# Single-token attention on one core: a first load in halves, a later one whole, one copy whole, one scaling on another engine, shorter column groups, and one load cut at row 120

## The chip, the cores and the metric

One core of a Trainium2 chip. The metric is device time in microseconds (us), median of several executions. The kernel before takes 1254.63 us. Its first three executions lie within 0.1 us of each other. "The span" is the stretch from the first to the last instruction in the trace; a run's time is 1.7 to 1.9 us longer.

## The reference

```python
B, H, Sq, Skv, Dh = 8, 32, 1, 4096, 128        # bfloat16 q, k, v
scale = Dh ** -0.5
scores = jnp.einsum('bhqd,bhkd->bhqk', q, k) * scale
attn = softmax(scores, axis=-1)
return jnp.einsum('bhqk,bhkd->bhqd', attn, v)
```

256 heads with one query each. Every byte of K and V (537 MB together) is read once.

## The kernel before

Heads are worked off in 32 tiles of 8. A tile of K or V is `[128 partitions, C = 256 positions, 128]`, 64 KB in each partition, 8.4 MB in all. VectorE multiplies K by q, TensorE sums over d, ScalarE takes exponentials, TensorE multiplies the weights by V. There is one V buffer and two K buffers; the last V goes into a K buffer. The loads and the tail:

```python
    cuts = {
        ("k", 0): [C // 4, C // 4, C // 2],
        ("k", NT - 4): [C // 2] * 2,
        ("k", NT - 3): [C // 2] * 2,
        ("k", NT - 2): [C // 2] * 2,
        ("k", NT - 1): [C // 4, C // 4, C // 2],
        ("v", NT - 1): [C // 2, C // 4, C // 8, C // 16, C // 32, LAST, LAST],   # LAST = 4
    }
    def load(kind, t):
        # ... choose buffer ...
        c0 = 0
        for n in cuts.get((kind, t), [C]):
            nc.sync.dma_start(buf[:, c0 : c0 + n, :], src[t, :, c0 : c0 + n, :])
            c0 += n
            if kind == "k" and t == 0 and c0 == n:
                nc.sync.dma_start(q_all[:], q_n)          # q goes behind the first piece
# ...
    def values_of(t, lo, hi):
        # weights x V, 4 positions a matmul, into one of four groups of 32 columns
        group = [
            0 if t == NT - 1 and C // 2 <= c0 < 3 * C // 4 else c0 // CB % TG
            for c0 in range(0, end, CB)
        ]
# ...
    def copy_of(t):                                       # PSUM -> SBUF, in bf16
        n = CB if t < NT - 1 else CB // 2
        nc.scalar.activation(out=comb[:, 0:n, :], in_=av[:, 0:n, :], func=ACT.Copy)
        if n < CB:
            nc.vector.tensor_copy(out=comb[:, n:CB, :], in_=av[:, n:CB, :])
# ...
    def finish_of(n):                                     # divide by the sum of weights, store
        nc.scalar.activation(out=stages[s][:, u, :], in_=ops.pop(n)[:], func=ACT.Copy,
                             scale=rzs.pop(n)[:, 0:1])
        # ... nc.scalar.dma_start(out ...)
```

The end runs so: the seven pieces of the last V land, the last values are multiplied, the last four positions (`w_last`) go straight into the result, the values are copied, four matmuls with `pick` collect them (`result_of`), the result is scaled and stored.

Of the kernel before, what the change touches and what calls it, by code (L numbers as in the profile page):

```python
# [7 lines left out]
ACT = mybir.ActivationFunctionType  # L8
ALU = mybir.AluOpType
# [6 lines left out]
TG = 4  # L16
# [7 lines left out]
def kernel(  # L24
# [7 lines left out]
    nc = tc.nc  # L32
    B, H, Sq, D = q.shape
    S = k.shape[2]
    P = nc.NUM_PARTITIONS
# [3 lines left out]
    C = S // PH  # L39
    NT = NH // G  # L40
    scale = float(D) ** -0.5
# [4 lines left out]
    CB = 4  # L46
    RG = R * G
    NQ = NT // R
# [28 lines left out]
        out=ident[:], in_=ident[:], pattern=[[-1, P]], compare_op=ALU.not_equal,  # L77
# [6 lines left out]
        out=heads[:], in_=heads[:], pattern=[[-1, G], [0, PH]], compare_op=ALU.not_equal,  # L84
# [6 lines left out]
        out=own[:], in_=own[:], pattern=[[-PH, G]], compare_op=ALU.is_ge,  # L91
# [3 lines left out]
        out=own[:], in_=own[:], pattern=[[PH, G]], compare_op=ALU.is_ge,  # L95
# [5 lines left out]
        out=same[:].rearrange("p (h x) -> p h x", x=PH),  # L101
        in_=own[:].rearrange("p (b h) -> p h b", h=TB // PH)
# [7 lines left out]
    for j in range(TG):  # L110
        part = pick[j * AG : (j + 1) * AG, :, :, :]
        nc.gpsimd.affine_select(
            out=part, in_=part, pattern=[[-G, CB], [G, R], [-1, RG]],
# [3 lines left out]
            out=part, in_=part, pattern=[[-G, CB], [0, R], [0, RG]],  # L117
# [3 lines left out]
            out=part, in_=part, pattern=[[G, CB], [0, R], [0, RG]],  # L121
# [7 lines left out]

    loads = {}  # L130
    cuts = {
        ("k", 0): [C // 4, C // 4, C // 2],
        ("k", NT - 4): [C // 2] * 2,
        ("k", NT - 3): [C // 2] * 2,
        ("k", NT - 2): [C // 2] * 2,
        ("k", NT - 1): [C // 4, C // 4, C // 2],
# [3 lines left out]
    def load(kind, t):  # L140
        src = k_t if kind == "k" else v_t
        home = "v" if kind == "v" and t < NT - 1 else "k"
        pool = k_pool if home == "k" else v_pool
        buf = pool.tile([P, C, D], BF16, name=f"{kind}t", tag=home)
        c0 = 0
        for n in cuts.get((kind, t), [C]):
            nc.sync.dma_start(buf[:, c0 : c0 + n, :], src[t, :, c0 : c0 + n, :])  # L147
            c0 += n
            if kind == "k" and t == 0 and c0 == n:
                nc.sync.dma_start(q_all[:], q_n)  # L150
        assert c0 == C
        loads[kind, t] = buf
# [88 lines left out]
    def values_of(t, lo, hi):  # L241
        vt = loads["v", t]
        w = ws[t]
        if lo == 0:
            avs[t] = ps_v.tile([P, CB * D], F32, name="av", tag="av")
        end = C if t < NT - 1 else C - LAST


        group = [
            0 if t == NT - 1 and C // 2 <= c0 < 3 * C // 4 else c0 // CB % TG  # L250
            for c0 in range(0, end, CB)
        ]
        for c0 in range(lo, hi, CB):
            i = c0 // CB
            j = group[i]
            nc.tensor.matmul(  # L256
                avs[t][j * AG : (j + 1) * AG, :], lhsT=w[:, c0 : c0 + CB, :],
                rhs=vt[:, c0 : c0 + CB, :], start=(i < TG), stop=(j not in group[i + 1 :]),
            )

    ops = {}
    zps = {}
    rzs = {}
    stages = {}
# [15 lines left out]
    def copy_of(t):  # L280
        comb = small.tile([P, CB, D], BF16, name="comb", tag="comb")
        av = avs.pop(t)[:].rearrange("p (m d) -> p m d", d=D)
        n = CB if t < NT - 1 else CB // 2
        nc.scalar.activation(out=comb[:, 0:n, :], in_=av[:, 0:n, :], func=ACT.Copy)  # L284
        if n < CB:
            nc.vector.tensor_copy(out=comb[:, n:CB, :], in_=av[:, n:CB, :])  # L286
        combs[t] = comb

    def result_of(t):
# [16 lines left out]
    def finish_of(n):  # L306
        s, u = divmod(n, OB)
        if u == 0:
            stages[s] = o_pool.tile([RG, OB, D], BF16, name="stage", tag="stage")
        nc.scalar.activation(  # L310
            out=stages[s][:, u, :], in_=ops.pop(n)[:], func=ACT.Copy, scale=rzs.pop(n)[:, 0:1]
        )
        last = s == NQ // OB - 1
        if u == OB - 1 or (last and u == OB - 2):
            lo = u if (last and u == OB - 1) else 0
            nc.scalar.dma_start(o_n[s, :, lo : u + 1, :], stages[s][:, lo : u + 1, :])

    Q = C // 4
    load("k", 0)
    with tc.manual_schedule():  # L320
        q_prep(0)
        for t in range(NT):
            v_last = t >= NT - 2
            n = t // R - 1
            if t + 1 < NT:
                load("k", t + 1)
            load("v", t)
            product(t, 0, Q)
            sum_over_d(t, 0)
            if t > 2 and t % R == 1:  # L330
                recip_of(n)
                finish_of(n)
# [5 lines left out]
            if t > 0 and not v_last:  # L338
                values_of(t - 1, 0, C)
                copy_of(t - 1)  # L340
# [6 lines left out]
            if t > 0 and v_last:  # L347
                values_of(t - 1, 0, C)
            scores_of(t, 3)
            weights_of(t)  # L350
            if t > 0:
                if v_last:
                    copy_of(t - 1)
                if t % R == 0:
                    norm_of(n)
                result_of(t - 1)
        values_of(NT - 1, 0, C // 2)
        norm_of(NQ - 1)
        recip_of(NQ - 1)
        values_of(NT - 1, C // 2, C - LAST)  # L360
        copy_of(NT - 1)
        result_of(NT - 1)
        finish_of(NQ - 1)


# [28 lines left out]
```

## Time and profile before

| | before |
|---|---|
| time, median | 1254.63 us (1254.58 to 1254.67) |
| span | 1252.8 us |
| DMA engines busy | 9 tenths or more in 39 of 40 slices |
| VectorE / TensorE / ScalarE busy | 77% / 44% / 27% |
| mean granted TensorE clock | 0.685 |

The load stream bounds the kernel; every other engine has time to spare. The lines of the profile are in the prediction. Each view has its own form: the chain of waits gives start, length and what was waited for or executed, and is read from the bottom up; the DMA view of a window gives packets, megabytes and the share that these packets took of sixteen engines' time.

### The profile page before, as it was taken

What the parts mean: (1) busy time and instruction counts of PE and PEld (TensorE: products, weight loads), DVE (VectorE), ACT (ScalarE), POOL (GpSimd) and SP (SyncE); (2) the same over time, 40 slices, a digit from 0 to 9 for tenths busy, and PEclk for the clock granted to TensorE, in tenths of its full rate; (3) what the DMA queues carried; (4) which work ended last, traced back from release to release, by engine and by line L of the source; (5) the groups of instructions that cost most, each with busy time, mean ns of one, the idle gap of its engine ahead of it and who ended that gap; (6) DMA issues with size and microseconds to landing.
All of it is one profiled execution on the core that took longest, in us unless ns stands there. A gap on an engine that the chain in (4) does not pass through costs nothing.

```text
span 1252.8 us, 8134 instructions
## 1 busy us (share of the span) xinstructions
PE 554.0 (44%) x3299; PEld 202.6 (16%) x3299; DVE 967.6 (77%) x531; ACT 343.3 (27%) x625; POOL 6.0 (0%) x26
## 2 busy tenths in 40 slices
PE   2444543345534355333453334542445434545356
PEld 0111111111111111111111111111112111211112
DVE  7877887777977779777797777886778877977981
ACT  0333123331233321333213333123330333311333
POOL 1000000000000000000000000000000000000000
PEclk8667666667657767576765776666676766676777
DMA  9999999999999999999999999999999999999997
GB/s 404 435 436 432 434 435 433 434 432 434 435 434 436 434 429 429 431 432 433 434 434 436 430 436 436 436 434 435 432 427 427 437 433 432 434 420 431 430 439 311
DMA packets 11734, 537.53 MB, mean 429 GB/s; under 512 B 1840, under 2 KB 2096, under 8 KB 2352
## 3 DMA queue, kind: packets, MB, share of 16 engines
q1 hardware_dynamic: 11360, 536.94, 99.3%
q8 instruction: 26, 0.43, 0.1%
q10 hardware_dynamic: 336, 0.07, 0.0%
q14 instruction: 12, 0.10, 0.0%
HBM read 536.94 MB, written 0.07 MB: 429 GB/s over the span
## 4 chain that ended last, share of the span: by engine, by line
DMA 79%; PE 14%; DVE 6%; issue 0%; SPq 0%; another core or an unknown queue 0%; ACT 0%
DMA vt<-in_v_dram 78%; PE av L256 13%; DVE kt L175 3%; DVE kt L178 2%; PE ps L190 1%; DMA q_all<-in_q_dram 1%; DVE sc L202 0%; SPq L147 0%; DVE pmax L212 0%; DVE spread L214 0%; DVE nmax L219 0%; DVE comb L286 0%; ACT comb L284 0%; ACT stage L310 0%
## 5 line engine op out<-in xcount | busy, mean ns | idle before, releaser
L175 DVE TENSOR_TENSOR kt<-kt,qb 128x8192 bf16<-128x8192 bf16 x128 | 565.2, 4415 | 181.9 <-DMA kt<-in_k_dram 175.3
L190 PE MATMUL ps<-kt,ident 128*128 128x512 bf16 x1024 | 353.6, 508 | 572.1 <-DVE kt L178 572.1
L231 ACT ACTIVATE w<-sc,bias 128x256 bf16<-128x256 f32 x256 | 300.5, 1587 | 260.5 <-DVE bias L223 260.5
L178 DVE TENSOR_TENSOR kt<-kt 128x4096 bf16<-128x4096 bf16 x128 | 293.4, 2292 | 4.4
L190 PEld LDWEIGHTS <-ident 128*128 128x128 bf16 x1024 | 119.6, 119 | 775.5 <-issue 506.1
L256 PE MATMUL av<-vt,w 128*32 128x512 bf16 x2047 | 176.5, 513 | 90.0 <-DMA vt<-in_v_dram 90.0
L202 DVE TENSOR_REDUCE sc<-ps 128x64 f32<-128x512 f32 x128 | 87.8, 686 | 68.1 <-PE ps L190 68.1
L284 ACT ACTIVATE comb<-av 128x512 bf16<-128x512 f32 (+1 forms) x32 | 19.5, 609 | 413.1 <-PE av L256 413.1
L231 ACT ACTIVATION_READ_ACCUMULATOR w<-sc,bias 128x1 f32 x256 | 126.6, 495 | 0.0
L256 PEld LDWEIGHTS <-w 128*32 128x32 bf16 x2047 | 68.7, 125 | 207.1 <-DMA vt<-in_v_dram 107.8
L163 ACT ACTIVATE qg<-qh 8x128 bf16<-8x128 f32 x32 | 8.5, 266 | 165.9 <-PE qh L159 165.9
L310 ACT ACTIVATE stage<-op,rz 16x128 bf16<-16x128 f32 x16 | 5.9, 371 | 56.4 <-DVE rz L276 41.3
L301 PE MATMUL op<-comb,pick 128*16 128x128 bf16 x128 | 13.4, 230 | 12.8 <-ACT comb L284 12.4
L212 DVE TENSOR_REDUCE pmax<-sc 128x1 f32<-128x256 f32 x32 | 13.4, 420 | 1.1
L165 PE MATMUL qp<-qg,heads 8*128 8x128 bf16 x32 | 7.5, 235 | 12.7 <-ACT qg L163 12.7
L276 DVE RECIPROCAL rz<-zp 16x1 f32<-16x1 f32 x16 | 2.4, 149 | 13.9 <-PE zp L268 13.9
L159 PE MATMUL qh<-q_all,ident 128*8 128x128 bf16 x32 | 8.2, 256 | 8.3 <-DMA q_all<-in_q_dram 8.3
L167 ACT ACTIVATE qb<-qp 128x128 bf16<-128x128 f32 x32 | 8.9, 277 | 10.4 <-PE qp L165 10.4
L301 PEld LDWEIGHTS <-pick 128*16 128x16 bf16 x128 | 7.6, 91 | 21.0 <-issue 20.9
L214 DVE TENSOR_SCALAR spread<-same,pmax 128x32 f32<-128x32 f32 x32 | 7.7, 241 | 1.1
L223 DVE TENSOR_SCALAR bias<-own,nmax 128x8 f32<-128x8 f32 x32 | 7.4, 231 | 1.1
L219 DVE TRANSPOSE_TENSOR_REDUCE nmax<-spread 128x1 f32<-128x32 f32 x32 | 6.8, 211 | 1.1
(27 smaller groups left out, 20.1 us busy)
## 6 DMA issues: line engine op xcount, KB each, us to landing
kt<-in_k_dram SPq DMA_DIRECT2D x8, 4096.0 KB, 43.0
kt<-in_k_dram SPq DMA_DIRECT2D x4, 2048.0 KB, 23.3
vt<-in_v_dram SPq DMA_DIRECT2D x1, 4096.0 KB, 41.4
vt<-in_v_dram SPq DMA_DIRECT2D x1, 2048.0 KB, 45.9
vt<-in_v_dram SPq DMA_DIRECT2D x1, 1024.0 KB, 47.8
vt<-in_v_dram SPq DMA_DIRECT2D x1, 512.0 KB, 48.6
vt<-in_v_dram SPq DMA_DIRECT2D x31, 33.3
kt<-in_k_dram SPq DMA_DIRECT2D x27, 47.4
```

The lines of the kernel that those rows point to most:

```text
L159: nc.tensor.matmul(qh[:], lhsT=ident[:, p0 : p0 + G], rhs=q_all[:, x, :], start=True, stop=True)
L163: nc.scalar.activation(out=qg[:], in_=qh[:], func=ACT.Copy)
L167: nc.scalar.activation(out=qb[:, 0, :], in_=qp[:], func=ACT.Copy)
L175: nc.vector.tensor_tensor(out=part, in0=part, in1=qb[:].to_broadcast([P, MC, D]), op=ALU.mult)
L178: nc.vector.tensor_tensor(out=part[:, :, 0 : D // 2], in0=part[:, :, 0 : D // 2], in1=part[:, :, D // 2 : D], op=ALU.add,)
L190: nc.tensor.matmul(ps[:], lhsT=ident[:], rhs=kt[:, u * UC : (u + 1) * UC, s * DS : (s + 1) * DS], start=(s == 0), stop=(s == n - 1),)
L202: nc.vector.tensor_reduce(out=scs[t][:, u * UC : (u + 1) * UC], in_=sums.pop((t, u))[:], axis=AX.X, op=ALU.add)
L212: nc.vector.tensor_reduce(out=pmax[:], in_=sc[:], axis=AX.X, op=ALU.max)
L231: nc.scalar.activation(out=w[:, :, g], in_=sc[:], func=ACT.Exp, bias=bias[:, g : g + 1], scale=scale, accum_out=esum[:, t % R, g : g + 1],)
L256: nc.tensor.matmul(avs[t][j * AG : (j + 1) * AG, :], lhsT=w[:, c0 : c0 + CB, :], rhs=vt[:, c0 : c0 + CB, :], start=(i < TG), stop=(j not i ...
L284: nc.scalar.activation(out=comb[:, 0:n, :], in_=av[:, 0:n, :], func=ACT.Copy)
L301: nc.tensor.matmul(ops[n][:], lhsT=pick[:, m, r, :], rhs=comb[:, m, :], start=(r == 0 and m == 0), stop=(r == R - 1 and m == CB - 1),)
```

## The change

The intent: fewer DMAs where cutting no longer helps, a shorter tail after the last load, and relief for the one DMA engine that comes last.

```diff
     cuts = {
-        ("k", 0): [C // 4, C // 4, C // 2],
-        ("k", NT - 4): [C // 2] * 2,
+        ("k", 0): [C // 2] * 2,
@@ load
-            nc.sync.dma_start(buf[:, c0 : c0 + n, :], src[t, :, c0 : c0 + n, :])
+            for p0, p1 in ((0, P - 8), (P - 8, P)) if kind == "v" and n == C // 32 else ((0, P),):
+                nc.sync.dma_start(buf[p0:p1, c0 : c0 + n, :], src[t, p0:p1, c0 : c0 + n, :])
@@ values_of
-            0 if t == NT - 1 and C // 2 <= c0 < 3 * C // 4 else c0 // CB % TG
+            0 if t == NT - 1 and C // 2 <= c0 < C // 2 + 3 * C // 16 else c0 // CB % TG
@@ copy_of
-        n = CB if t < NT - 1 else CB // 2
-        nc.scalar.activation(out=comb[:, 0:n, :], in_=av[:, 0:n, :], func=ACT.Copy)
-        if n < CB:
-            nc.vector.tensor_copy(out=comb[:, n:CB, :], in_=av[:, n:CB, :])
+        nc.scalar.activation(out=comb[:], in_=av, func=ACT.Copy)
@@ finish_of
-        nc.scalar.activation(out=stages[s][:, u, :], ..., func=ACT.Copy, scale=rzs.pop(n)[:, 0:1])
+        if n == NQ - 1:
+            nc.vector.tensor_scalar(out=stages[s][:, u, :], in0=ops.pop(n)[:],
+                                    scalar1=rzs.pop(n)[:, 0:1], scalar2=None, op0=ALU.mult)
+        else:
+            nc.scalar.activation(...)                     # as before
```

The diff also takes away the cut of the K of tile 28 (`NT - 4`).

More of the change, by code (lines that the diff above doesn't have):

```diff
@@ L309, in finish_of @@
             stages[s] = o_pool.tile([RG, OB, D], BF16, name="stage", tag="stage")
-        nc.scalar.activation(
-            out=stages[s][:, u, :], in_=ops.pop(n)[:], func=ACT.Copy, scale=rzs.pop(n)[:, 0:1]
-        )
+        if n == NQ - 1:
+            nc.vector.tensor_scalar(
+                out=stages[s][:, u, :], in0=ops.pop(n)[:], scalar1=rzs.pop(n)[:, 0:1],
+                scalar2=None, op0=ALU.mult,
+            )
+        else:
+            nc.scalar.activation(
+                out=stages[s][:, u, :], in_=ops.pop(n)[:], func=ACT.Copy,
+                scale=rzs.pop(n)[:, 0:1],
+            )
         last = s == NQ // OB - 1
```

## The prediction

The sum is 0.64 + 0.13 + 0.04 = 0.81 us, so 1253.82 us. What the term of 0.64 rested on is the assumption, which no trace of before shows, that the 120-row part leaves out the engine that comes last. That engine would then lose its eight packets, 80 ns apart, and the landings from 1246.9 to 1248.00 that the text gives follow from this. Rival (1) is that another engine is left out.

> **What bounds the kernel now.** I read the page first, then the chain of waits, the timeline of both ends, the DMA view in short windows, and at last the trace's single records (matmuls, DMA packets, and the sixteen landing marks of each DMA). From the page:
>
> ```profile
> DMA  9999999999999999999999999999999999999997
> ...
> DMA 79%; PE 14%; DVE 6%; issue 0%; SPq 0%; another core or an unknown queue 0%; ACT 0%
> ```
>
> K and V are read once, 537 MB by the page, and the DMA engines are busy in every slice but the last. In the inner slices they move about 434 GB/s, and 537 MB at 434 GB/s is 1237 us of the 1252.8 us span. No part of the change removes bytes, so only what lies outside that stream can move: about 1.8 us before the first packet (the first starts at 1.83 us) and the end. The chain of waits at the end (start, length, what, in us):
>
> ```profile
> 1199.17 48.80 DMA vt<-in_v_dram
> 1247.97 0.04 issue
> 1248.02 0.73 PE av L256 x3
> 1248.77 0.39 ACT comb L284
> 1249.16 0.02 issue
> 1249.19 0.44 DVE comb L286
> 1249.62 0.04 issue
> 1249.67 0.29 PE op L301 x2
> ```
>
> The 8-column piece of the last V lands at 1247.97, and then 2.4 us of small work follow (the last step, not shown, is ScalarE's scaling at 1249.97); the store and the closing waits take another 2.4 us (issue at 1250.36, span end 1252.77). The DMA view of three short windows near the end, 1244 to 1245, 1246 to 1247 and 1247 to 1248 us (packets, MB, share of 16 engines):
>
> ```profile
> q1 hardware_dynamic: 60, 0.25, 59.8%
> ...
> q1 hardware_dynamic: 151, 0.16, 43.8%
> ...
> q1 hardware_dynamic: 22, 0.03, 7.1%
> ```
>
> 7.1% is one engine in sixteen: the last microsecond is one engine working alone. The sixteen landing marks of the 8-column piece say the same: six engines at 1241.70 to 1242.69, nine at 1246.13 to 1246.87, one at 1247.97. The lone engine's packets of this piece are 8 of 2,048 bytes, 80 ns apart, from 1246.90 to 1247.54; two more pieces of 8 packets of 1,024 bytes follow, 43 ns apart. So the end is set by **one late engine**, 1.1 us behind the next.
>
> Why it is late shows too. The page lists 26 instruction packets (16,384 bytes each); following packets by their ends, each fetch lengthens one load packet beside it by about 0.5 us, eight different engines take turns, and the last fetch before the end (1231.87 us) falls on the engine that comes last. I expect the same fetches after[...].
>
> [...]
>
> **Part by part.**
>
> *First K in halves, instead of two quarters and a half.* The first product needs the first piece and q behind it. It started at 9.57; a quarter is 2.1 MB, 4.8 us at 434 GB/s, so now it starts near 14.4. That moves VectorE by 4.8 us in the first two tiles. SP's own issues before:
>
> ```profile
> 40.98 0.33 SPq L147 DMA_DIRECT2D kt<-in_k_dram  x1
> 66.73 0.33 SPq L147 DMA_DIRECT2D vt<-in_v_dram  x1
> 73.91 0.33 SPq L147 DMA_DIRECT2D kt<-in_k_dram  x1
> ```
>
> The third K goes out at 40.98 while the first V lands only at 61.6, so at 45.8 it is still early. The second V needs the first values done: near 70 instead of 66.7, while the third K transfers until 80.6. The fourth K moves from 73.9 to at most 78.7, needed at 100. No gap in the stream: 0.
>
> *K of tile 28 whole.* The name in the diff is the fourth from last. VectorE's multiplies of tiles 27 and 28 began:
>
> ```profile
> 1053.09 4.42 DVE L175 TENSOR_TENSOR kt<-kt,qb 128x8192 bf16<-128x8192 bf16 x1 [6.90 <-DMA kt<-in_k_dram]
> ...
> 1084.89 4.42 DVE L175 TENSOR_TENSOR kt<-kt,qb 128x8192 bf16<-128x8192 bf16 x1
> ```
>
> Whole tiles land every 38.7 us, so tile 28 starts at 1091.8, 6.9 us later. But in tile 28 VectorE waited 6.1 us at 1118.95 behind values that need a V, so its end moves only about 3 us (1122.5 to 1125.5), and tile 29 waits 6.6 us in the same place (1157.1), so it ends where it did. The K loads behind are issued some 25 us ahead of need. Cost: 0.
>
> *The 120 and 8 split.* [...] The piece then lands with the next engines, 1246.9 plus at most one packet of 0.08; the last two pieces land at 1247.68 and 1248.00 instead of 1248.32 and 1248.64. Its semaphores shift, so the last piece now waits for the V before it to land (1227.9): 20 us early enough.
>
> *Column groups.* In one group matmuls start 0.216 us apart; in four groups, four start together. Before, 16 from 1243.69 plus three of the later pieces ran in a line until 1247.57, 0.2 us after the landing of the 16-column piece (1247.33). With 12 in line and 4 spread, all before that piece has started by 1246.75. The work then follows the landings: 1247.37 for four, 1247.58 for two, 1247.72 for the last (before: 1248.36). By itself the part is worth nothing, since the old kernel waits at 1248.02 anyway; with earlier landings it keeps about 0.07 us from being lost.
>
> *Copy and scaling.* By shape (mean ns after the comma):
>
> ```profile
> L284 ACT ACTIVATE comb<-av 128x512 bf16<-128x512 f32 x31 | 19.1, 617 | 402.8 <-PE av L256 402.8
> ...
> L286 DVE CAST comb<-av 128x256 bf16<-128x256 f32 x1 | 0.4, 424 | 6.6 <-ACT comb L284 6.6
> ```
>
> The halves were meant to run side by side and ran one after the other: VectorE waited for ScalarE. From the last value's end to the last result matmul's end that took 1.20 us (1248.735 to 1249.938). A whole copy takes 0.597 in 29 of 31 cases (the mean holds two of 0.90 right after exponentials); with 0.04 ahead, 0.05 behind, four result matmuls 0.055 apart (0.165) and 0.217 for the last, 1.07: **0.13 saved**. The last scaling on ScalarE took 0.357 in the timeline. VectorE's reciprocal of one element from PSUM took 0.149 and its 256-element cast 0.424, so about 0.28 for 128 elements, perhaps 0.36 with a pointer scalar (bias, 8 elements, takes 0.231): estimate 0.32, **0.04 saved**. The store is issued from ScalarE's queue, which now waits for another engine, at the 0.03 us it waited before.
>
> Sum[...]: 0.64 + 0.13 + 0.04 = 0.81 us. Times of whole runs stand 1.85 us over the span and move with it: 1254.63 - 0.81 = 1253.82.
>
> **Rivals.** (1) [...] Then the landing stays[...], and only 0.17 us remain: 1254.5. I give this 1 in 4. (2) Starting later opens a gap in the stream, because K tile 28 or the first K now frees a buffer late: each gap would cost its length, up to 5 us, 1259. The margins above (some 10 us at the start, 25 at tile 28) speak against it. (3) TensorE, not the landing, is the bound at the end: then the groups part would give the gain, and the split none. The wait at 1248.02 for the landing speaks against it.
>
> **Range.** The three runs before lie within 0.1 us, so differences of half a microsecond are real on one chip. I mix 0.81 (3 in 4) and about 0.15: 1253.9. The range, 1253.0 to 1255.0, holds both outcomes and a little of another chip. 2% is 25 us, thirty times anything in the sum: within 2% is nearly sure.
>
> **What would show it.** Right: first product near 14.4, tile 28 multiplied from about 1091.8, and yet a last V landing no later; the lone engine's tail before 1248 shorter by 0.64; the last value near 1247.7; one copy of 0.60; store issued near 1249.55. Wrong: the last landing unchanged (the engine is another), a DMA share under 9 in an inner slice (a gap), or a VectorE scaling over 0.40 us.

## The result, and the profile after

The changed kernel took 1255.3 us (1255.09 to 1255.53, 6 runs), the kernel before 1254.64 (1254.58 to 1254.67, 6 runs). The ratio is 1.0005 (95% interval 0.9992 to 1.0018). The interval does not separate the two; the runs do, since the ranges don't touch. The change **costs** about 0.7 us, where 0.7 us was to be saved, and 1255.3 lies outside the range.

The chain of waits of the changed kernel at its end (start, length, what):

```profile
1199.12 49.84 DMA vt<-in_v_dram
...
1249.00 0.70 PE av L256 x3
...
1249.72 0.61 ACT comb L283
...
1250.37 0.40 PE op L298 x4
...
1250.79 0.34 DVE stage L308
```

Set it beside the same chain of before: the last three value matmuls begin at 1249.00 and not at 1248.02. The piece whose landing they wait for comes 0.99 us later. The last step of before, which the prediction does not show, was

```profile
1249.97 0.36 ACT stage L310
```

From the values on, the tail is shorter: 1249.00 to 1251.13 (end of the scaling) is 2.13 us, before it was 1248.02 to 1250.33, 2.31 us.

The groups by shape say the same of the two steps that changed engine or size:

```profile
L283 ACT ACTIVATE comb<-av 128x512 bf16<-128x512 f32 x32 | 19.7, 616 | 407.3 <-PE av L256 407.3
...
L308 DVE TENSOR_SCALAR stage<-op,rz 16x128 bf16<-16x128 f32 x1 | 0.3, 339 | 7.2 <-PE op L298 7.2
```

The DMA view of windows 1244 to 1245, 1246 to 1247, 1247 to 1248 and 1248 to 1249 us after (the first three answer to those of before):

```profile
q1 hardware_dynamic: 58, 0.24, 57.9%
...
q1 hardware_dynamic: 149, 0.18, 69.8%
...
q1 hardware_dynamic: 73, 0.07, 22.9%
...
q1 hardware_dynamic: 20, 0.02, 6.5%
```

Between 1246 and 1247 the engines are busy for 69.8% of their time and not 43.8%, for hardly more bytes (0.18 MB against 0.16). They are not idle, they are slow. One engine alone (6.5%) still works in a microsecond that before was nearly empty (1.0% from 1248 to 1249.5 us). TensorE shows the consequence; its timeline:

```profile
1248.40 0.40 PE L256 MATMUL av<-vt,w 128*32 128x512 bf16 x4 [0.90 <-DMA vt<-in_v_dram]
1249.00 0.69 PE L256 MATMUL av<-vt,w 128*32 128x512 bf16 x3 [0.20 <-DMA vt<-in_v_dram]
```

It idles 0.90 us for the 16-column piece, a piece that the change does not touch. So the delay is there before the cut piece. The trace keeps, for each DMA, the times at which its semaphore was counted up, sixteen for a whole one; they are called landing marks here. The last mark of each piece of the last V:

```text
columns of the piece    before     after
128                     1238.72    1238.69
 64                     1243.65    1243.96
 32                     1246.07    1246.59
 16                     1247.33    1248.36
  8 (120 rows after)    1247.97    1248.96
  8 (8 rows)               -       1247.63
  4                     1248.32    1249.27
  4                     1248.64    1249.58
```

Up to 1238.7 the streams are alike, so neither the first K nor tile 28 left a mark there. Then two stretches lose time. The view by windows (length, busy times of the engines, clock, DMA share, GB/s) of 1240.5 to 1242.0, before and then after:

```profile
1240.50:1242.00 1.50, 1.50 (x20) 0.83 (x13) 0.00 (x0) 0.00 (x0) 0.00 (x0) 0.50 0.95 380
```

```profile
1240.50:1242.00 1.50, 1.50 (x20) 0.84 (x16) 0.00 (x0) 0.00 (x0) 0.00 (x0) 0.50 0.99 304
```

Busier (0.99 against 0.95) and slower (304 against 380 GB/s): a fifth less. In single records, the late engine's 16,384-byte packets, 611 to 619 ns each before, took 740, 844 and 656 ns here. In the second stretch, 1246.0 to 1247.5, six of its 4,096-byte packets took 188 to 382 ns instead of 159. These extras add up to 0.39 + 0.57 = 0.96 us. The cut piece is moved in packets of 2,048 bytes. They start from 1240.33 to 1242.44 on the engines that are early and from 1245.46 to 1246.93 on the nine in the middle, and each of the two stretches overlaps one of these.

The records carry no engine number, but the landing marks tell which engines are which. The 120-row DMA has one mark at its issue (1199.73) and fifteen later, the 8-row DMA eight later. Of the fifteen, five are early, nine in the middle, one late. All sixteen are six, nine and one. So the engine that gets nothing is one of the **early** ones. The 8-row part's eight marks are four early and four in the middle; the late engine is not among them. It still has its eight packets of 2,048 bytes (1247.83 to 1248.39, 80 ns apart).

The start and tile 28 answered much as predicted. What SP (SyncE, which issues the loads) issued after:

```profile
45.94 0.33 SPq L147 DMA_DIRECT2D kt<-in_k_dram  x1
69.35 0.33 SPq L147 DMA_DIRECT2D vt<-in_v_dram  x1
79.37 0.33 SPq L147 DMA_DIRECT2D kt<-in_k_dram  x1
```

and VectorE's first multiply and the first of tile 28:

```profile
14.54 4.42 DVE L175 TENSOR_TENSOR kt<-kt,qb 128x8192 bf16<-128x8192 bf16 x1 [11.58 <-ACT qb L167]
...
1091.89 4.42 DVE L175 TENSOR_TENSOR kt<-kt,qb 128x8192 bf16<-128x8192 bf16 x1 [6.81 <-DMA kt<-in_k_dram]
```

### The profile page after: what moved, and what is told of

The parts are those of the page before. It is cut to its first block, busy times and chain, and to the rows that moved or that the text cites. A ratio compares the mean times of both kernels' runs of the same rounds, so it can differ in the third digit from the quotient of the medians. Undisturbed runs are those within 1.5% of the kernel's fastest.

```text
span 1253.5 us, 8130 instructions
## 1 busy us (share of the span) xinstructions
PE 553.9 (44%) x3299; PEld 201.7 (16%) x3299; DVE 967.5 (77%) x531; ACT 343.1 (27%) x624; POOL 6.0 (0%) x26
## 4 chain that ended last, share of the span: by engine, by line
DMA 79%; PE 15%; DVE 6%; issue 0%; SPq 0%; ACT 0%
DMA vt<-in_v_dram 78%; PE av L256 13%; DVE kt L175 3%; DVE kt L178 2%; PE ps L190 1%; DMA q_all<-in_q_dram 1%; DVE sc L202 0%; SPq L147 0%; DVE pmax L212 0%; ACT comb L283 0%; DVE spread L214 0%; DVE nmax L219 0%; PE op L298 0%; DVE stage L308 0%; ACT qb L167 0%
## 5 line engine op out<-in xcount | busy, mean ns | idle before, releaser
L283 ACT ACTIVATE comb<-av 128x512 bf16<-128x512 f32 x32 | 19.7, 616 | 407.3 <-PE av L256 407.3
```

The costliest lines, as they stand in the source:

```text
L283: nc.scalar.activation(out=comb[:], in_=av, func=ACT.Copy)
```

## The experiments

The theory (P), as far as runs can test it: when a load is cut in rows, which rows of SBUF are written at the same time decides how long its packets take, and packets of other DMAs that run beside it take longer too. The mechanism behind this was not shown by any run. The rivals were the shifted compute, the additional DMA, and the number of engines used.

**1. Without the split.** The changed kernel, with

```diff
-            for p0, p1 in ((0, P - 8), (P - 8, P)) if kind == "v" and n == C // 32 else ((0, P),):
-                nc.sync.dma_start(buf[p0:p1, ...], src[t, p0:p1, ...])
+            nc.sync.dma_start(buf[:, c0 : c0 + n, :], src[t, :, c0 : c0 + n, :])
```

> The changed kernel with the 8-column piece whole again; all else of the change stays. Theory P ([...]packets that run at the same time get slower): the 16-column piece of the last V lands near 1247.3 again and not at 1248.36, the 4,096-byte packets take 159 ns throughout, and the time is 1254.63 less the 0.15 that the copy (1.20 to 1.07) and the scaling (0.357 to 0.339) save: 1254.5. Rival K (the shifted start or the whole K of tile 28 moved the stream or the phase of the compute against it): stays at 1255.2 to 1255.4.

1254.28 us (1254.08 to 1254.38, 4 runs) against 1254.49 of before (1254.46 to 1254.63, 7 runs), ratio 0.9998. The loss is gone, and about 0.2 us is saved. The last three values start at 1248.12, and the stretch 1240.5 to 1242.0 runs at 373 GB/s again:

```profile
1240.50:1242.00 1.50, 1.50 (x20) 0.77 (x16) 0.00 (x0) 0.00 (x0) 0.00 (x0) 0.50 0.93 373
```

Whatever the split costs, the rest of the change does not cost it.

**2. The split alone**, in the kernel before (the same lines added).

> The kernel before with the 120 and 8 split alone. Theory P: the last landings come about 1.0 us later as in the changed kernel, and nothing is saved in the tail: 1255.4 to 1255.7. Rival K: as before, 1254.6, or 1254.0 if the split does what the prediction said.

1255.53 us (1255.38 to 1256.24, 4 runs), before 1254.49, ratio 1.0009: about 1.0 us lost, and the 8-column piece lands at 1249.00 (120 rows). So the split alone brings the loss, and the rival of the shifted compute falls. The profiled execution was the slowest, 1256.24, for a reason of its own. TensorE's timeline there:

```profile
1244.16 6.16 PE L257 MATMUL av<-vt,w 128*32 128x512 bf16 x31 [2.02 <-DMA vt<-in_v_dram]
```

31 matmuls in one run without a gap of note, from 1244.16 to 1250.32. Single records show the ones in a line 0.43 us apart for about 3 us instead of 0.216, so in this execution TensorE itself was late. The trace has the reason: the granted TensorE clock (the third column from the right) was about half in that stretch. The view of 1245 to 1248 us, run 2 and then before:

```profile
1245.00:1248.00 3.00, 3.00 (x9) 1.04 (x8) 0.00 (x0) 0.00 (x0) 0.00 (x0) 0.51 0.53 188
```

```profile
1245.00:1248.00 3.00, 2.95 (x23) 1.27 (x22) 0.00 (x0) 0.00 (x0) 0.00 (x0) 1.00 0.38 143
```

That raised the question of runs 13 and 14.

**3. As many DMAs, but whole rows.** Run 1 with the 8-column piece as two of 4 columns:

```diff
-        ("v", NT - 1): [C // 2, C // 4, C // 8, C // 16, C // 32, LAST, LAST],
+        ("v", NT - 1): [C // 2, C // 4, C // 8, C // 16, C // 64, C // 64, LAST, LAST],
```

> The changed kernel with the 8-column piece as two pieces of 4 columns, each over all 128 rows: the same number of DMAs as with the split[...]. Theory P: as without the split, 1254.4 to 1254.7. Rival N (one DMA more, its issue held back until 1227.8, its descriptors and semaphore cost the time): 1255.2 or more.

1254.20 us (1254.16 to 1254.43, 4 runs), ratio 0.9998. One DMA more costs nothing.

**4. The split at 112 and 16 rows.** The changed kernel with

```diff
-            for p0, p1 in ((0, P - 8), (P - 8, P)) if ...
+            for p0, p1 in ((0, P - 16), (P - 16, P)) if ...
```

> The changed kernel with the split at 112 and 16 rows[...]. Theory P: slower than without the split by about as much as the 120 and 8 split, 0.6 to 1.2 us over it: 1255.1 to 1255.7. Rival E (what costs is that 15 and 8 engines are used instead of 16): as without the split, 1254.5.

1255.35 us (1255.07 to 1256.1, 4 runs), ratio 1.0009. As slow as 120 and 8, so the loss does not hang on these two numbers. How many engines each part used here was not shown; that it isn't a matter of fifteen engines instead of sixteen is shown by run 5 below, where all are busy (0.98) and yet slow.

**5 to 8. The cost made large.** Run 1 with the whole V of tile 16, in the middle of the stream, cut in rows. `parts` is the only thing that differs:

```diff
+            parts = PARTS if kind == "v" and t == NT // 2 else [slice(0, P)]
+            for rs in parts:
+                nc.sync.dma_start(buf[rs, c0 : c0 + n, :], src[t, rs, c0 : c0 + n, :])
# run 5: [slice(0, P // 2), slice(P // 2, P)]
# run 6: [slice(0, P - 8), slice(P - 8, P)]
# run 7: [slice(32 * h + r, 32 * h + 32, 4) for h in range(4) for r in range(4)]   8 rows, 4 apart
# run 8: [slice(8 * h, 8 * h + 8) for h in range(16)]                              8 rows in sequence
```

> The changed kernel without the split at the end, but with the whole V of tile 16 in the middle of the kernel loaded as rows 0 to 63 and rows 64 to 127, to see the suspected cost large. [...] Theory P: [...]these packets take about 4.8 us instead of 2.42 and the kernel some 19 us longer (8.39 MB at half of 434 GB/s). [...]

> The same with rows 0 to 119 and 120 to 127 of the V of tile 16. Theory P: most packets of that load take between 2.42 and 4.8 us or more, and the kernel is 10 to 29 us longer. Rival E (only the share of rows per engine counts[...]): 2.4 us longer at most.

> The same V of tile 16 as 16 DMAs of 8 rows each, taken 4 rows apart (rows 0, 4, ... 28 of each 32), so that each is moved by 8 engines[...]. Theory P: packets stay at 2.42 us, but only 8 engines work: 38.8 us instead of 19.3, the kernel about 19 us longer (1274).

> The same as 16 DMAs of 8 consecutive rows. [...]only the order of rows differs. Theory P: [...]packets take about 9.7 us, and the kernel is about 135 us longer (16 packets of 9.7 us instead of 19.3 us). A theory in which the number of engines alone counts: as with rows 4 apart, 1274.

One look each (state unknown), with 1254.62 us for before on the same chip: 1278.07 (64 and 64), 1283.84 (120 and 8), 1288.8 (8 rows 4 apart), 1331.3 (8 rows in sequence). The view by windows, 662 to 682 us, while that V loads; the last two columns are the DMA share and GB/s. First run 1, where it is whole, then runs 5, 6, 7 and 8:

```profile
662.00:682.00 20.00, 7.60 (x18) 2.39 (x18) 17.22 (x7) 6.23 (x13) 0.00 (x0) 0.50 1.00 430
```

```profile
662.00:682.00 20.00, 4.02 (x11) 1.42 (x12) 13.49 (x6) 6.03 (x13) 0.00 (x0) 0.58 0.98 204
```

```profile
662.00:682.00 20.00, 3.98 (x10) 1.37 (x11) 12.87 (x5) 6.44 (x13) 0.00 (x0) 0.55 0.99 204
```

```profile
662.00:682.00 20.00, 7.26 (x18) 2.33 (x18) 17.45 (x7) 6.00 (x13) 0.00 (x0) 0.59 0.47 198
```

```profile
662.00:682.00 20.00, 4.51 (x12) 1.59 (x13) 13.92 (x7) 7.57 (x15) 0.00 (x0) 0.50 0.46 96
```

Runs 5 and 6 keep all engines busy and move less than half the bytes: a 65,536-byte packet took 5.1 and 5.0 us (medians, 670 to 680 us) instead of 2.42. The rate fell to less than half (204 against 430 GB/s).

Runs 7 and 8 are the pair to compare. The same number of engines is busy (share 0.47 and 0.46, eight of sixteen), for rows of the same size; only which rows go together differs. With rows 4 apart the packets took 2.42 us, with rows in sequence mostly 4.8 to 5.2. The forecasts were off in size. Run 5 lost 23.5 us, where 19 were forecast (and none by the rival). Run 8 was to have 9.7 us a packet and 135 us lost, an estimate. It had half that in this window, and lost 76.7 us. The eight landing marks of one of its DMAs lie 7 to 8 us apart, more than one packet; why its packets took half of the estimate is not settled. From 720 us, with the next K beside it, its packets took 7.2 us (median). And run 7 lost 34 us, not 19: the next K was issued at 688.05, while that V was still being loaded. From 690 to 700 us all engines are busy (share 1.06) at 223 GB/s, and the packets took 5.0 us too. That is the tail's case seen large: while cut rows are written, the packets of a whole DMA beside them are slow as well.

**9 and 10. SBUF side or HBM side?** In runs 7 and 8 the rows read from HBM changed with the rows written. These two part them, and give a wrong result (relative error 0.14):

```diff
+            for rs, rd in zip(to, of):
+                nc.sync.dma_start(buf[rs, c0 : c0 + n, :], src[t, rd, c0 : c0 + n, :])
# run 9:  to = 8 rows in sequence, of = 8 rows 4 apart;   run 10: the reverse
```

> As the run with 16 DMAs of 8 consecutive rows, but only the rows written in SBUF are consecutive; those read from HBM are 4 apart. The result is wrong on purpose: the V rows of tile 16 land in other places. Theory P[...]: as with consecutive rows, 65,536-byte packets of 4.7 to 5.2 us from the start of that load, about 1331 us. Rival H (the order in which HBM is read makes the packets slow): as with rows 4 apart, 2.42 us in its first half, about 1289 us.

> The reverse, also wrong on purpose: rows written in SBUF 4 apart, rows read from HBM consecutive. Theory P: 2.42 us in the first half of that load and about 5 us later, when the other engines load the next K; about 1289 us. Rival H: 4.7 to 5.2 us throughout and about 1331 us.

1330.33 and 1288.78 us. The same window, run 9 and then run 10:

```profile
662.00:682.00 20.00, 4.19 (x11) 1.46 (x12) 13.66 (x6) 6.13 (x13) 0.00 (x0) 0.57 0.48 100
```

```profile
662.00:682.00 20.00, 7.45 (x18) 2.37 (x18) 17.25 (x7) 6.12 (x13) 0.00 (x0) 0.59 0.47 198
```

Each goes with the rows that it writes, to within a microsecond of runs 8 and 7. The order of reading plays no part that can be seen. The cost goes with the rows written in SBUF.

**11. The two K changes alone**, in the kernel before (the `cuts` lines of the diff).

> The kernel before with the two K changes alone (first K in halves, K of tile 28 whole). By the prediction: no gap in the stream and no change, within 0.1 us of before, though the first product starts at 14.5 instead of 9.57. A rival for which the start or the phase matters: 0.3 us or more off.

1254.40 us (1254.27 to 1254.47, 5 runs), before 1254.60 (1254.51 to 1254.99, 9 runs), ratio 0.9998. Nothing lost, as predicted; rather 0.2 us gained, more than the 0.1 expected. The trace shows only 0.07 us of it: its last value starts 0.05 us *later* than before (1248.40 against 1248.36), and from the store's issue to the span's end it takes 0.12 us less (2.28 against 2.40). Why, and where the rest is, I leave open.

**12. Copy and scaling alone**, in the kernel before (those lines of the diff).

> The kernel before with the whole copy and the scaling on VectorE alone. By the prediction's sum for these two, corrected by the 0.339 us that the scaling took: 0.13 + 0.02 = 0.15 us less than before, 0.10 to 0.20.

1254.43 us (1254.37 to 1254.47, 5 runs) against the same 1254.60: 0.17 us saved, as worked out.

**13 and 14. The column groups.** Run 1, and the changed kernel, each with the old line:

```diff
-            0 if t == NT - 1 and C // 2 <= c0 < C // 2 + 3 * C // 16 else c0 // CB % TG
+            0 if t == NT - 1 and C // 2 <= c0 < 3 * C // 4 else c0 // CB % TG
```

> The changed kernel without the split and with the old column groups (16 last values in one group instead of 12). By the prediction the groups part is worth nothing as long as the landings are where they were, because the last values wait for the 8-column piece: 1254.2 to 1254.4, as without the split. Rival G (16 in one line delay the end, as the profile of the split alone suggests, where the line ran at 0.43 us a matmul instead of 0.216): 1254.5 or more, and a wider spread of its runs.

> The changed kernel, split and all, with the old column groups. If TensorE grants its full clock, the line of 16 ends near 1247.9, before the late 16-column piece at 1248.4: 1255.3, as the changed kernel. Rival G: in some runs the line itself sets the end, up to 1256.2 as in one run of the split alone, with a median of 1255.5 or more.

1254.29 us without the split (1254.06 to 1254.48, 5 runs; run 1 had 1254.28 on another occasion), 1255.39 with it (1255.17 to 1255.49, 5 runs), before 1254.53. No difference either way. No time like that of run 2's profile came back in five runs; run 4 had one of 1256.1 with the new groups. So the groups are worth nothing that these runs show. But the clock at the end was 1.00 from 1245 us on in the profiles of both, so what a shorter line in one group saves at half clock, the case of run 2, was not measured.

One more figure separates all runs at the tail. In the stretch 1240.5 to 1242.0 the four kernels with cut rows (the change, runs 2, 4 and 14) moved 304, 310, 282 and 306 GB/s; the six with whole rows there (before, runs 1, 3, 11, 12 and 13) moved 363 to 388.

A version that beats both kernels is the change without the split: 1254.20 to 1254.29 us in runs 1, 3 and 13, some 0.2 to 0.3 us under before, with ranges that do not touch in runs 1 and 3. The two gains of runs 11 and 12 (0.20 and 0.17) do not add up in it (0.21), which is within the spread of such runs.

## Why the prediction was wrong

- *The stream bounds the kernel:* right, and right that one late engine sets the end. But "only what lies outside that stream can move" failed: the cut rows slowed the stream itself, 304 GB/s against 380 in the stretch above.
- *Why an engine is late:* right in kind. Following packets again, each of 25 fetches during the loads took its engine about 1.0 to 1.1 us, and then the next load packet took about 0.5 us more (most 2.88 to 2.97 us instead of 2.42); the prediction read the 0.5 alone. The 26th fetch comes after the last load packet. The page after lists 26 instruction packets again, and 3,299 matmuls and 3,299 weight loads, as before.
- *First K and tile 28 cost nothing:* right, with one bound passed and one size off. First product 14.54 (near 14.4), second V issued at 69.35 (near 70), fourth K at 79.37 (at most 78.7, a little over, needed at 100), tile 28 at 1091.89 (1091.8), its end 1.1 us later (the next multiply at 1123.64, before 1122.52) and not 3. Run 11 shows no loss.
- *Copy:* right. From the last value's end to the last result matmul's end 1.07 us (1249.686 to 1250.753), as predicted to the hundredth; 1.20 before.
- *Scaling:* right in kind; 0.339 us where 0.32 was estimated, so 0.02 saved instead of 0.04. Run 12 shows 0.17 for both.
- *Column groups:* right that they are worth nothing by themselves. The 0.07 that they were to keep could not be seen, since the earlier landings did not come. The line's 0.216 us a matmul held at the granted clock of 1.00 that before had there: run 2's profile has 0.43 at 0.51.
- *The split: this step failed, twice.* First, it took the engine that is left out for the late one, which would lose 8 packets of 80 ns, 0.64 us. The engine left out was an early one, and the late one kept its eight packets. The prediction gave this 1 in 4 as rival (1). Second, and worse, neither the sum nor any rival had a term for what the two parts do to *other* transfers. Rival (1) said that the landing "stays", or comes one packet of 0.08 us later; it came 0.99 later. The missing term is what cut rows cost the packets beside them: 0.96 us of longer packets on the late engine, and 0.9 to 1.1 us in time whenever rows are cut at the end (runs 2 and 4 against before, the change against run 1, run 14 against run 13). A check was at hand: the prediction asked how many engines the parts use and which, and not where their rows lie.
- *The sum, as it came out:* the last values' start moved by +0.95 (1248.359 to 1249.309), copy -0.14, scaling -0.02, together +0.79; the store was issued 0.80 later, the span grew by 0.7, and the time by 0.66.
- *The range:* the mix of 0.81 (3 in 4) and 0.15 is 0.65, so 1253.98 and not 1253.9; that changes nothing here. The range held rival (1) in the size that I had given it, and left nothing for a loss of more than 0.4 us.

Open: whether the late engine could be relieved at all; no run here shows it. Open too: by what mechanism rows that are written together slow each other down. The runs show that it goes with the rows written in SBUF, and not why.

## What to carry to other kernels

In these runs a load cut in rows was not a smaller version of the whole one: packets of 65,536 bytes took 5.0 to 5.1 us instead of 2.42 (runs 5 and 6), and packets of whole DMAs beside cut rows got longer too (up to 382 ns instead of 159 in the tail of the changed kernel). Cut loads along the free dimension: a piece cut so cost nothing (run 3, 1254.20 us against 1254.28). Before taking work off the engine that comes last, find out which engine that is; the number of marks of a DMA with few engines tells it, and a look at the busy share beside GB/s (0.99 and 304 against 0.95 and 380) tells slow engines from idle ones.
